# A speech joint kernel on one core: the first batch's projection by w_f as two groups of seven block products

## The chip, the core and the metric

The kernel runs on one core of a Trainium2 chip. The metric is the device time of one execution in microseconds (us). A core has five engines that run side by side, each with its own queue in order: TensorE (PE in the profile, with its weight loads as PEld), VectorE (DVE), ScalarE (ACT), GpSimd (POOL) and SyncE (SP), which here issues the DMA transfers. They wait for one another through semaphores. Matrix products land in PSUM, in eight banks; everything else is in SBUF.

## What is computed

```python
B, T, D, K, U = 2, 4000, 512, 5, 8
for i in range(K):                      # first convolution over time, 5 taps
    h = h + einsum("btc,cd->btd", xp[:, i:i+T, :], w1[i])
h = gelu(h)[:, ::2, :]                  # every second step is kept: 2000
for i in range(K):                      # second convolution
    f = f + einsum("btc,cd->btd", hp[:, i:i+T1, :], w2[i])
f = gelu(f)[:, ::2, :]                  # 1000 steps
fe = einsum("btd,de->bte", f, w_f)      # the projection of this case
ge = einsum("bud,de->bue", g, w_g)
j = tanh(fe[:, :, None, :] + ge[:, None, :, :])
out = einsum("btud,dv->btuv", j, w_o)   # 2 x 1000 x 8 x 512
```

Inputs and output are bf16.

## The kernel before

**Order by a planner.** The body records operations with their reads, writes and an assumed cost in a `Plan` (L69). `edges` (L109) finds which operation must wait for which; `schedule` (L160) and `once` (L228) place them: in each step the engine that can start first takes an operation that is ready. TensorE, SP and Pool take the one recorded first, ACT and DVE the one with the earliest due time. `learn` (L195) moves due times where TensorE has gaps, in up to 150 passes. `emit` (L280) then writes each engine's queue in that fixed order, so on the chip the queues run in order. Operations recorded with `flex` (L90) may go to either of two engines, as the planner finds. `pl.port` marks operations for a rule at L262 to L267: DVE and Pool instructions that are marked do not overlap in the plan, and a marked DVE operation close behind another marked one is charged 0.2 us more.

**Layout.** All features lie with their 512 channels as four blocks of 128 partitions (index k) and time along the free axis. fT[b] holds the second convolution's output of batch b, four blocks of 3 x 334 steps (three residues r, 334 steps each); feT[b] holds fe in f32, four blocks of 1002 steps.

**Stages.** Start-up: `turn` (L575) turns the first rows of x by TensorE and evicts each of four turns in two halves, half 0 on DVE and half 1 on ACT; `direct` (L752) computes the first part of the first convolution from them. Meanwhile `w1part` and `w2part` (L599 and L616) form sums of the convolution weights, on DVE (`tensor_tensor`, `scalar_tensor_tensor`) with scalings on ACT. The convolutions then run as `Triple`s and `Unit`s: a unit is one block of 128 output channels of a part of the time axis, in five steps s1 to s5 of 4 or 8 matmuls of up to 334 columns, with ACT copies (`sd`) and DVE sums between them that free the unit's PSUM bank for its next step. Units 0 to 15 are the first convolution, 16 to 19 the second one of batch 0, 20 to 23 that of batch 1. The main loop (L887) interleaves the steps of neighbouring units and, by `when(slot, ...)`, other work: `load_late` (slot 17) loads w_f, w_g and w_o; `tail_zero` zeroes the end of hT on Pool; `w2part` runs in slots 9 to 13.

**Around the change.** w_f is used by `fe(b, half, m)` (L801): four matmuls of 501 columns into a bank (block m of the output, one half of the time axis), evicted into feT by ACT for odd m and DVE for even m. Batch 0 takes all eight of them in a row behind one convolution step (L1087 to L1092); those of batch 1 stand at the end of the list `conv` of convolution steps that are left, and `piece(n)` takes the next n from that list. The output stage works on j in column blocks of 128. `Seven` (L958) computes four of them, 512 columns of j by 512 outputs, as seven block products: the 2 x 2 blocks of j and of w_o are added and subtracted beforehand (`sums` into ss on DVE or Pool, `wosums` at L843 into tw on Pool), products 1 to 7 of 4 matmuls of 256 columns go to PSUM, some are kept in SBUF (`keep`, into sn), and four outputs are evictions or DVE sums with a kept one. `Plain` (L935) is the direct product of one block of 128. `tanhs` records the ACT tanhs that fill j ahead of the products (rings of 12 and 10 blocks of 256 columns). The loop at L1110 goes over 28 groups of seven; `fill` says what goes between: two convolution steps for each of the first nine groups, one for the next six, then a plain block.

**Buffers.** tw lies over w_g. w_f, w_g and w_o lie over w1_x, so their loads wait for its last use. wv holds f32 sums of w1 from the start-up, ssum and ws those of w2.

Of the kernel before, what the change touches and what calls it, by code (L numbers as in the profile page):

```python
# [12 lines left out]
P = 128  # L13
# [55 lines left out]
class Plan:  # L69
# [158 lines left out]
    def once(self, pred, succ, late, hold):  # L228


        ops, HOP, n = self.ops, self.HOP, len(self.ops)
        left = [len(p) for p in pred]
        ready = list(hold)
        free = {e: 0.0 for e in ("pe", "act", "dve", "pool", "sp")}
        cand = {e: [] for e in free}
        engines = [o.alt or (o.eng,) for o in ops]
        for i in range(n):
            if not left[i]:
                for e in engines[i]:
                    cand[e].append(i)  # L240
        order, where = {e: [] for e in free}, {}
        wire, lock, start, done = 0.0, 0.0, [0.0] * n, [0.0] * n
        for _ in range(n):
            best = None
            for e, c in cand.items():
                if c:
                    t = max(free[e], min(ready[i] for i in c))
                    if best is None or t < best[0]:
                        best = (t, e)
            t, e = best  # L250
            now = [i for i in cand[e] if ready[i] <= t + 0.02]
            i = min(now) if e in ("pe", "sp", "pool") else min(now, key=lambda i: (late[i], i))
            for f in engines[i]:
                cand[f].remove(i)
            order[e].append(i)
            o = ops[i]
            cost = o.cost
            if o.alt:
                where[i], cost = e, o.alt[e][1]
            start[i] = t  # L260
            free[e] = t + cost
            if o.port:  # L262
                if lock > t - 0.2 and e == "dve":
                    free[e] = max(t, lock) + cost + 0.2
                elif lock > t:
                    free[e] = lock + cost
                lock = free[e]  # L267
            done[i] = end = free[e]
            if o.dma:
                wire = max(wire, t + 1.8) + o.wire  # L270
                end = max(wire, t + 2.0) + o.slack
            for s in succ[i]:
                ready[s] = max(ready[s], end + HOP if pred[s][i] else free[e])
                left[s] -= 1
                if not left[s]:
                    for f in engines[s]:
                        cand[f].append(s)
        return max(free.values()), order, start, done, ready, where
# [76 lines left out]
def bass_standalone__seq2seq_rnn_t_joint__speech_kernel(  # L355
# [40 lines left out]
    with ExitStack() as es:  # L396
        cur = [16512]

        def at(name, shape, dtype, offset=None):
            o = cur[0] if offset is None else offset  # L400
            b = Buf(nc, name, shape, dtype, o)
            if offset is None:
                cur[0] = (b.end + 31) // 32 * 32
            return b
# [54 lines left out]
        assert ss[3].end <= xs[2].end and ss[7].end <= xs[1].end  # L459
        tw = at("tw", [4, 2, NT // 2], FP16, wg_sb.end - wg_sb.bytes)  # L460
        assert tw.end <= wg_sb.end
        ps = Psum(es.enter_context(nc.psum_tensor("acc", [P, 8 * NT], FP32)))
        block = es.enter_context(nc.Block(no_gpsimd_drain=True))
        pl = Plan(nc)
# [9 lines left out]
        def tt(eng, o, a, b, op):  # L474
            pl.op(eng, lambda e: e.tensor_tensor(out=o.ap, in0=a.ap, in1=b.ap, op=op), (a, b), (o,),  # L475
                  0.02 + 2.14e-3 * o.ap.free_size() if eng == "pool" else vec_cost(o, (a, b)))
# [98 lines left out]
        def turn(rt, pp, cost):  # L575
            for h in range(2):
                bk = 4 * (rt ^ pp) + 2 * h + 1
                pv = View(psb[:, bk * 1024:bk * 1024 + 512].rearrange("p (r k c) -> p r k c", r=2, k=2), np.array([bk]), True)

                def fn(e, pv=pv, h=h):  # L580
                    for k in range(2):
                        for r in range(2):
                            ins = e.transpose(pv.ap[:, r, k, :], xr[rt].h[:, 2 * r + pp, 2 * h + k, :], ident.h[:, :])
                    return ins
                pl.op("pe", fn, (xr[rt][:], ident[:]), (pv,), cost)
                lo = 16 + 2 * P * rt
                o = eo[pp, 2 * h:2 * h + 2, lo:lo + 2 * P].map(lambda a: a.rearrange("p k (c r) -> p k c r", r=2))
                v = pv.map(lambda a: a.rearrange("p r k c -> p k c r"))
                if h:
                    act(o, v, ACT.Copy)  # L590
                else:
                    pl.op("dve", lambda e, o=o, v=v: e.tensor_copy(out=o.ap, in_=v.ap), (v,), (o,), vec_cost(o, (v,)))
# [42 lines left out]
        class Triple:  # L635
# [5 lines left out]
            def __init__(self, z, off, r, w, out, n=NT3, home={}):  # L641
                self.HOME = {**self.HOME, **home}
                self.z_, self.off, self.r_, self.w, self.out, self.n = z, off, r, w, out, n
# [31 lines left out]
            def product(self, which, m, bank, start):  # L675
                at_z, i = self.HOME[which]
                w, p = self.w[which]
                n = self.n
                mm(ps.cols(bank * NT, n),
                   [(w[p, k, m * P:(m + 1) * P],  # L680
                     self.z_[i, k, self.off:self.off + n] if at_z else self.r_[i, k, 0:n]) for k in range(NK)],
                   start, True, False)
# [118 lines left out]
        def fe(b, half, m):  # L801
            q = NT3 // 2
            v = ps.cols(bank(), 3 * q)
            mm(v, [(wf_sb[k, m * P:(m + 1) * P], fT[b][k, :, half * q:(half + 1) * q]) for k in range(NK)], True, True)
            v = v.map(lambda a: a.rearrange("p (r q) -> p q r", r=3))
            o = feT[b][m, 3 * half * q:3 * (half + 1) * q].map(lambda a: a.rearrange("p (q r) -> p q r", r=3))
            if m % 2:
                act(o, v, ACT.Copy)
            else:
                pl.op("dve", lambda e, o=o, v=v: e.tensor_copy(out=o.ap, in_=v.ap), (v,), (o,), vec_cost(o, (v,)))  # L810

        def slot(j):
            if j < XB:
                return jT, j % RING
            j = (j - XB) % (WIDE + RING)
            return (jX, j) if j < WIDE else (jT, j - WIDE)
# [23 lines left out]
                act(jcols(k, lo, n), feT[b][k, t:t + n], ACT.Tanh, bias=geT[k * BU + v:k * BU + v + 1])  # L840
                lo += n

        def wosums():  # L843
            h = NT // 2
            b11, b12, b21, b22 = (wo_sb[2 * k:2 * k + 2, c * h:(c + 1) * h] for k in range(2) for c in range(2))
            tt("pool", tw[0], b12, b11, sub)
            tt("pool", tw[1], b22, tw[0], sub)
            tt("pool", tw[2], b22, b12, sub)
            tt("pool", tw[3], b21, tw[1], sub)

        def tail_zero(b):
            v = hT[b][2:6, :, HOFF + NT3 - 1:HOFF + NT3]
# [6 lines left out]
        def when(slot, *what):  # L859
            fixed.setdefault(slot, []).extend(what)  # L860

        def steps(slot, i, lo, hi):
            when(slot, *[lambda w=w: trip[i].step(w) for w in STEPS[lo:hi]])
# [18 lines left out]
        when(17, load_late, lambda: tail_zero(1))  # L882
        steps(18, 5, 0, 4)
        steps(19, 5, 4, 13)
        when(20, ge)
        nu = 21
        for t in range(nu):  # L887
# [23 lines left out]
        def take():  # L911
            return free.pop(0)
# [45 lines left out]
        class Seven:  # L958
# [12 lines left out]
            def a(self, r, k):  # L971
                return jcols(slice(2 * k, 2 * k + 2), self.c[r], H)
# [30 lines left out]
            def keep(self, eng, bk):  # L1003
                v = sn[Seven.kept % len(sn)]
                Seven.kept += 1
                evict(eng, v[:], ps.cols(bk * NT, NT))
                return v
# [53 lines left out]
        def tanhs(upto, read, more=0):  # L1061

            while pend:
                v, k = pend[0]
                room = all(owner(j) < 0 or (owner(j) + 1) * JB <= read for j in range(v * T2 // JB, -(-(v + 1) * T2 // JB)))
                if v * T2 >= upto:
                    if not more or not room or v >= U and not far[0]:
                        break
                    more -= 1
                assert room, (v, upto, read)  # L1070
                tanh(*pend.pop(0))
# [8 lines left out]
        def piece(n=1):  # L1080
            for _ in range(n):
                if conv:
                    conv.pop(0)()
                    far[0] = not conv

        wosums()
        first = [lambda h=h, m=m: fe(0, h, m) for m in range(NK) for h in range(2)]  # L1087
        piece()
        for i, f in enumerate(first):
            f()  # L1090
            if i % 2:
                tanhs(0, 0, 1)  # L1092
        piece(3)

        S1 = 15
        gaps = (1, 3, 5, 7)
# [78 lines left out]
```

## Time and profile before

| what | value |
|---|---|
| median of three runs | 254.28 us (253.91 to 254.64) |
| profiled execution, its own time | 253.94 us |
| its span, first to last instruction | 252.2 us |
| TensorE clock granted | 1.000 |
| projection of batch 0, 32 matmuls of 501 columns | 120.35 to 127.17 us |
| w_o sums on Pool, four | 118.31 to 122.9 us, 1.15 us each |
| issue of w_f's load, time to landing | 90.63 us, 3.6 us |
| first output products | 130.01 us; first group of seven about 132 us |
| last tanh ends, last matmul starts | about 232 us, 248.7 us |

A profile page lists busy time by engine, then forty slices of the span with a digit for the busy share of each (9 is 90% or more), then the chain of work that ended last, followed back from the end. Rows of a timeline show start, duration, engine, line of the code, operation, and output <- inputs with their shapes. An instruction's duration runs from its issue, so it may contain a wait for a resource that the profile doesn't name.

### The profile page before, as it was taken

How to read it: one execution, taken by the hardware profiler on the slowest of the kernel's cores; microseconds unless marked ns; L12 is line 12 of the kernel's file. 1: busy time of each engine (PE TensorE's matmuls, PEld its weight loads, DVE VectorE, ACT ScalarE, POOL GpSimd, SP SyncE). 2: the span in 40 equal slices, each digit the busy share in tenths (PEclk: the TensorE clock that was granted, in tenths of full speed). 3: DMA queues.
4: the chain of work that ended last, by engine and by line, in shares of the span. 5: the costliest groups of instructions: out<-in, count | busy, mean ns of one | idle time of the engine just before them, and what ended most of it. 6: DMA issues, size and time to landing. Idle time of an engine off the chain costs nothing.

```text
span 252.2 us, 5270 instructions
## 1 busy us (share of the span) xinstructions
PE 246.4 (98%) x1913; PEld 180.9 (72%) x1919; DVE 209.9 (83%) x342; ACT 210.0 (83%) x352; POOL 103.2 (41%) x107
## 2 busy tenths in 40 slices
PE   7999999999999999999999999999999999999994
PEld 3745977666666666667467878877778878787882
DVE  2699999956999998295546799799899999999783
ACT  4396998859869767884699999999999999998762
POOL 1000000000000000002418889698998999998500
PEclk9999999999999999999999999999999999999999
DMA  6999999989100043000002223332344446555646
GB/s 233 306 229 188 172 142 179 187 148 358 45 0 3 0 143 110 0 1 3 0 0 86 83 87 99 130 108 83 118 137 149 145 135 205 165 167 170 205 149 209
DMA packets 55159, 31.99 MB, mean 127 GB/s; under 512 B 32062, under 2 KB 54878, under 8 KB 55134
## 3 DMA queue, kind: packets, MB, share of 16 engines
q1 hardware_dynamic: 54846, 31.47, 47.6%
q8 instruction: 15, 0.25, 0.4%
q10 hardware_dynamic: 288, 0.20, 0.3%
q14 instruction: 10, 0.08, 0.1%
HBM read 7.86 MB, written 16.38 MB: 96 GB/s over the span
## 4 chain that ended last, share of the span: by engine, by line
PE 87%; DVE 5%; DMA 4%; ACT 1%; issue 1%; SPq 0%; DVEq 0%
PE acc L488 87%; DMA w_sb<-in_w_dram 4%; DVE wu L595 1%; DVE row L475 1%; DVE xa L475 1%; DVE ssum L475 1%; DVE w_t L475 1%; DVE og L475 1%; ACT row L480 0%; DVE w_x L475 0%; ACT w_x L480 0%; ACT sd L480 0%; ACT hT L480 0%; SPq L511 0%; ACT ost L480 0%
## 5 line engine op out<-in xcount | busy, mean ns | idle before, releaser
L475 DVE TENSOR_TENSOR og<-acc,sn 128x512 bf16<-128x512 f32 x84 | 55.6, 683 | 6.4 <-PE acc L488 4.4
L480 ACT ACTIVATE jT<-feT,geT 128x1000 bf16<-128x1000 f32 (+6 forms) x56 | 52.7, 1016 | 0.5 <-DVE feT L810 0.4
L488 PE MATMUL acc<-tw,ss 128*128 128x256 f16 x336 | 46.0, 273 | 0.0
L488 PE MATMUL acc<-row,w_sb 128*128 128x334 bf16 (+2 forms) x224 | 38.8, 296 | 0.0
L488 PEld LDWEIGHTS acc<-tw,ss 128*128 128x128 f16 x336 | 32.6, 98 | 7.8 <-ACT sn L917 0.4
L917 ACT ACTIVATE sn<-acc 128x512 f32<-128x512 f32 x54 | 34.8, 657 | 3.8 <-PE acc L488 3.5
L980 POOL TENSOR_TENSOR ss<-jT 128x512 f16<-128x512 bf16 x23 | 28.8, 1263 | 13.4 <-ACT jT L480 10.8
L488 PE MATMUL acc<-wo_sb,jT 128*128 128x256 bf16 (+1 forms) x187 | 31.5, 292 | 0.3
L488 PEld LDWEIGHTS acc<-row,w_sb 128*128 128x128 bf16 x224 | 21.0, 97 | 8.9 <-DVE acc L595 0.4
L480 ACT ACTIVATE jX<-feT,geT 128x1000 bf16<-128x1000 f32 (+4 forms) x28 | 26.2, 986 | 0.0
L472 POOL MEMSET hT<- 128x8 bf16 (+2 forms) x6 | 0.8, 148 | 61.6 <-ACT hT L480 44.1
L480 ACT ACTIVATE hT<-acc 128x334 bf16<-128x334 f32 (+3 forms) x36 | 15.5, 441 | 9.7 <-PE acc L488 9.7
L488 PEld LDWEIGHTS acc<-wo_sb,jT 128*128 128x128 bf16 x192 | 18.7, 98 | 6.2
L595 DVE SCALAR_TENSOR_TENSOR acc<-acc,sd 128x334 f32<-128x334 f32 (+2 forms) x24 | 11.6, 483 | 13.8 <-PE acc L488 13.7
L480 ACT ACTIVATE sd<-acc 128x334 f32<-128x334 f32 (+2 forms) x48 | 20.4, 433 | 3.2 <-PE acc L488 2.4
L918 DVE COPY sn<-acc 128x512 f32<-128x512 f32 x30 | 20.5, 685 | 2.4 <-PE acc L488 2.4
L475 DVE TENSOR_TENSOR row<-row 128x1336 bf16<-128x1336 bf16 (+2 forms) x24 | 19.0, 795 | 0.0
L980 POOL TENSOR_TENSOR ss<-jX 128x512 f16<-128x512 bf16 x15 | 17.4, 1171 | 1.2 <-ACT jX L480 0.6
L488 PE MATMUL acc<-hT,w_t 128*128 128x334 bf16 x96 | 17.6, 304 | 0.0
L488 PE MATMUL acc<-xp,w_t 128*128 128x334 bf16 (+1 forms) x96 | 17.4, 305 | 0.0
L488 PE MATMUL acc<-xp,w_x 128*128 128x334 bf16 (+1 forms) x96 | 16.9, 305 | 0.0
L488 PE MATMUL acc<-eo,w_sb 128*128 128x468 bf16 (+2 forms) x96 | 16.2, 328 | 0.6 <-ACT eo L480 0.6
(111 smaller groups left out, 511.2 us busy)
## 6 DMA issues: line engine op xcount, KB each, us to landing
out_dram<-og SPq DMA_DIRECT2D x98, 128.0 KB, 2.0
w_sb<-in_w_dram SPq DMA_DIRECT2D x10, 512.0 KB, 5.5
out_dram<-ost SPq DMA_DIRECT2D x10, 128.0 KB, 2.2
xr<-in_x_dram SPq DMA_DIRECT2D x2, 512.0 KB, 4.6
wf_sb<-in_w_f_dram SPq DMA_DIRECT2D x1, 512.0 KB, 3.6
wg_sb<-in_w_g_dram SPq DMA_DIRECT2D x1, 512.0 KB, 4.6
wo_sb<-in_w_o_dram SPq DMA_DIRECT2D x1, 512.0 KB, 5.7
xp<-in_x_dram SPq DMA_TRANSPOSE x18, 4.9
```

What stands on the lines that cost most here:

```text
L472: pl.op("pool", lambda e: e.memset(v.ap, 0.0), (), (v,))
L475: pl.op(eng, lambda e: e.tensor_tensor(out=o.ap, in0=a.ap, in1=b.ap, op=op), (a, b), (o,), 0.02 + 2.14e-3 * o.ap.free_size() if eng == "po ...
L480: pl.op("act", lambda e: e.activation(o.ap, i.ap, func, scale=scale, bias=0.0 if bias is None else bias.ap), rd, (o,), o.ap.free_size() * ...
L488: ins = e.matmul(o.ap, lhsT=l.ap, rhs=r.ap, start=start and n == 0, stop=stop and n == len(pairs) - 1, skip_group_check=not check)
L595: pl.op(eng, lambda e: e.scalar_tensor_tensor(out=o.ap, in0=a.ap, scalar=f, in1=b.ap, op0=ALU.mult, op1=add), (a, b), (o,), vec_cost(o, (a ...
L917: pl.flex({"act": (lambda e: e.activation(o.ap, v.ap, ACT.Copy), 0.05 + n * 0.833e-3), "dve": (lambda e: e.tensor_copy(out=o.ap, in_=v.ap) ...
L918: "dve": (lambda e: e.tensor_copy(out=o.ap, in_=v.ap), 0.065 + n * 1.04e-3)}, (v,), (o,))
L980: fn = lambda e, o=S[i], x=x, y=y, op=op: e.tensor_tensor(out=o.ap, in0=x.ap, in1=y.ap, op=op)
```

## The change

Batch 0's projection no longer runs as eight `fe` calls. Two objects of a new class `FeSeven` compute it as 2 x 2 blocks: the rows are the two halves of the time axis (168 steps of each of three residues, overlapping by two steps), the inner blocks are halves of the 512 channels, and the columns are halves of the 512 outputs; t = 0 or 1 picks one block of 128 within each half. Each object has seven products of 2 matmuls of 504 columns, three kept results (kf, in f32 over ssum and ws) and four outputs. Two sets of sums go in: `fsums` on DVE from fT into sf (bf16, over row[0], four sums of 1008 elements), and `wsums(twf, wf_sb)` on Pool from w_f into twf (f16, over wv, four sums of 512 elements), recorded in slot 18 of the main loop, right after the loads. `wosums` becomes `wsums(tw, wo_sb)`; with `pl.hold` it waits for the last feature sum.

The steps of the remaining convolution that are recorded ahead of the output stage go from four to nine: piece(2), the first products, piece(3), the rest, piece(4). The same steps are then missing from the fill of the later groups. At the start-up, half 0 of the last turn goes to ACT instead of DVE. In the planner a marked operation directly behind another marked one of the same engine is no longer charged for the port.

```diff
-        wire, lock, start, done = 0.0, 0.0, [0.0] * n, [0.0] * n
+        wire, lock, owner, start, done = 0.0, 0.0, None, [0.0] * n, [0.0] * n
...
             if o.port:
-                if lock > t - 0.2 and e == "dve":
+                if owner != e and lock > t - 0.2 and e == "dve":
                     free[e] = max(t, lock) + cost + 0.2
-                elif lock > t:
+                elif owner != e and lock > t:
                     free[e] = lock + cost
-                lock = free[e]
+                lock, owner = free[e], e
...
+        QH = NT3 // 2 + 1
+        twf = at("twf", [4, 2, NT // 2], FP16, wv[2].end - wv[2].bytes)
+        sf = at("sf", [4, 2, 3, QH], BF16, xt_off + 8192)
+        kf = [at(f"kf{i}", [3, QH], FP32, v.end - v.bytes) for i, v in enumerate(ssum + ws[:2])]
...
-                if h:
+                if h or rt and pp:
                     act(o, v, ACT.Copy)
...
+        def fhalf(b, r, k):
+            q0 = r * (NT3 - QH)
+            return fT[b][k, :, q0:q0 + QH]
+
+        def fsums(b):
+            a = lambda r, k: fhalf(b, r, slice(2 * k, 2 * k + 2))
+            pl.port = True
+            tt("dve", sf[0], a(1, 0), a(1, 1), add)
+            tt("dve", sf[1], sf[0], a(0, 0), sub)
+            tt("dve", sf[2], a(0, 0), a(1, 0), sub)
+            tt("dve", sf[3], a(0, 1), sf[1], sub)
+            pl.port = False
+
+        class FeSeven:
...
+            def product(self, i, bk, start):
+                h, lo = NT // 2, self.t * P
+                rhs = {1: lambda k: fhalf(self.b, 0, k), 2: lambda k: fhalf(self.b, 0, 2 + k),
+                       4: lambda k: fhalf(self.b, 1, 2 + k)}.get(i)
+                if rhs is None:
+                    si = {5: 0, 6: 1, 7: 2, 3: 3}[i]
+                    rhs = lambda k: sf[si, k]
+                lhs = {1: lambda k: wf_sb[k, lo:lo + P], 2: lambda k: wf_sb[2 + k, lo:lo + P],
+                       3: lambda k: wf_sb[2 + k, h + lo:h + lo + P]}.get(i)
+                if lhs is None:
+                    ti = {5: 0, 6: 1, 7: 2, 4: 3}[i]
+                    lhs = lambda k: twf[ti, k, lo:lo + P]
+                mm(ps.cols(bk * NT, 3 * QH), [(lhs(k), rhs(k)) for k in range(2)], start, True, False)
...
+            def keep(self, bk):
+                v = kf[FeSeven.kept % len(kf)]
+                FeSeven.kept += 1
+                evict(None, v[:].map(lambda a: a.rearrange("p r q -> p (r q)")), ps.cols(bk * NT, 3 * QH))
+                return v
+
+            def out(self, r, c, bk, v=None):
...
+                if v is None:
+                    evict(None, o, p)
+                else:
+                    tt("dve", o, p, v[:].map(cut), add)
+
+            def p1(self):
+                self.A = take()
+                self.product(1, self.A, True)
+                self.s1 = self.keep(self.A)
+
+            def p2(self):
+                bk = take()
+                self.product(2, bk, True)
+                self.out(0, 0, bk, self.s1)
+                free.append(bk)
...
+            def p6(self):
+                self.product(6, self.A, False)
+                self.u2 = self.keep(self.A)
+
+            def p7(self):
+                self.product(7, self.A, False)
+                self.out(1, 1, self.A, self.d5)
...
-        def wosums():
+        def wsums(tw, w):
             h = NT // 2
-            b11, b12, b21, b22 = (wo_sb[2 * k:2 * k + 2, c * h:(c + 1) * h] for k in range(2) for c in range(2))
+            b11, b12, b21, b22 = (w[2 * k:2 * k + 2, c * h:(c + 1) * h] for k in range(2) for c in range(2))
+            pl.port = True
             tt("pool", tw[0], b12, b11, sub)
             tt("pool", tw[1], b22, tw[0], sub)
             tt("pool", tw[2], b22, b12, sub)
             tt("pool", tw[3], b21, tw[1], sub)
+            pl.port = False
...
         steps(19, 5, 4, 13)
+        when(18, lambda: wsums(twf, wf_sb))
...
-        wosums()
-        first = [lambda h=h, m=m: fe(0, h, m) for m in range(NK) for h in range(2)]
-        piece()
-        for i, f in enumerate(first):
-            f()
-            if i % 2:
-                tanhs(0, 0, 1)
+        piece(2)
+        f0, f1 = FeSeven(0, 0), FeSeven(0, 1)
+        f0.p1()
+        f0.p2()
+        fsums(0)
+        pl.hold = [pl.ops[-1].idx]
+        wsums(tw, wo_sb)
+        pl.hold = []
+        f1.p1()
+        f0.p5()
+        f1.p2()
+        f0.p6()
+        f1.p5()
+        f0.p7()
+        f0.p3()
+        f0.p4()
+        tanhs(0, 0, 1)
         piece(3)
+        f1.p6()
+        f1.p7()
+        f1.p3()
+        f1.p4()
+        tanhs(0, 0, 3)
+        piece(4)
```

In the built program's queues, Pool has the four w_f sums ahead of the zeroing of hT's tail; ACT has the scaling of the last w2 block ahead of a bank copy `sd` that stood ahead of it before; the eight calls' 32 matmuls become 28, with 44 more convolution matmuls between them and the first group of seven than before.

More of the change, by code (lines that the diff above doesn't have):

```diff
@@ L461, in bass_standalone__seq2seq_rnn_t_joint__speech_kernel @@
         assert tw.end <= wg_sb.end
+        QH = NT3 // 2 + 1
+        twf = at("twf", [4, 2, NT // 2], FP16, wv[2].end - wv[2].bytes)
+        sf = at("sf", [4, 2, 3, QH], BF16, xt_off + 8192)
+        kf = [at(f"kf{i}", [3, QH], FP32, v.end - v.bytes) for i, v in enumerate(ssum + ws[:2])]
+        assert twf.end <= wv[3].end and sf.end <= xt[0].end and 3 * QH <= NT
         ps = Psum(es.enter_context(nc.psum_tensor("acc", [P, 8 * NT], FP32)))
@@ new lines, in bass_standalone__seq2seq_rnn_t_joint__speech_kernel, with __init__, p5, p3 @@
+        class FeSeven:
+            def __init__(self, b, t):
+                self.b, self.t = b, t
+            def product(self, i, bk, start):
[11 more added lines that the diff above has]
+                mm(ps.cols(bk * NT, 3 * QH), [(lhs(k), rhs(k)) for k in range(2)], start, True, False)
+            kept = 0
+            def keep(self, bk):
[4 more added lines that the diff above has]
+            def out(self, r, c, bk, v=None):
+                q = NT3 // 2
+                cut = lambda a: a[:, :, r:r + q].rearrange("p r q -> p q r")
+                p = ps.cols(bk * NT, 3 * QH).map(lambda a: cut(a.rearrange("p (r q) -> p r q", r=3)))
+                o = feT[self.b][2 * c + self.t, 3 * r * q:3 * (r + 1) * q].map(lambda a: a.rearrange("p (q r) -> p q r", r=3))
+                if v is None:
[11 more added lines that the diff above has]
+                free.append(bk)
+            def p5(self):
+                self.D = take()
+                self.product(5, self.D, True)
+                self.d5 = self.keep(self.D)
+            def p6(self):
[4 more added lines that the diff above has]
+                self.out(1, 1, self.A, self.d5)
+            def p3(self):
+                self.product(3, self.D, False)
+                self.out(0, 1, self.D, self.u2)
+                free.append(self.D)
+            def p4(self):
+                self.product(4, self.A, False)
+                self.out(1, 0, self.A)
+                free.append(self.A)
```

## The prediction

> **What bounds the kernel now.** I read the first page from the top: busy time, the slices, then the chain of waits.
>
> ```profile
> span 252.2 us, 5270 instructions
> PE 246.4 (98%) x1913; PEld 180.9 (72%) x1919; DVE 209.9 (83%) x342; ACT 210.0 (83%) x352; POOL 103.2 (41%) x107
> ...
> PE   7999999999999999999999999999999999999994
> ...
> DVE  2699999956999998295546799799899999999783
> ...
> PE 87%; DVE 5%; DMA 4%; ACT 1%; issue 1%; SPq 0%; DVEq 0%
> ```
>
> TensorE is busy in every slice but the first and last, and holds 87% of the chain. So a matmul taken away shortens the kernel, and a stall put into TensorE's queue lengthens it, each one for one, unless the planner has another matmul ready. Next I cut the span into the stretches that the change touches (columns: length, then PE, PEld, DVE, ACT, POOL busy with counts, clock, DMA share, GB/s).
>
> ```profile
> 84.00:94.40 10.40, 10.40 (x75) 7.07 (x74) 10.40 (x19) 6.76 (x14) 0.00 (x0) 1.00 0.24 81
> 94.40:100.20 5.80, 5.80 (x43) 3.97 (x41) 5.50 (x12) 4.27 (x9) 0.00 (x0) 1.00 0.40 129
> 100.20:105.40 5.20, 5.20 (x39) 3.57 (x37) 0.01 (x1) 5.13 (x7) 0.17 (x1) 1.00 0.00 2
> ...
> 120.30:127.00 6.70, 6.70 (x34) 3.04 (x33) 3.65 (x6) 4.87 (x8) 2.55 (x3) 1.00 0.00 0
> ```
>
> The last row is the projection that the change rewrites: DVE and ACT have room there. The first two are where its new Pool work lands: Pool is empty, but DVE is full until 100.2, with the sums of the second convolution's weights. Then the DMA issues (time of issue 90.63, 3.6 us to landing for w_f), and for what happens when Pool and DVE work at once, the timeline of the output stage, and all DVE sums into `ss` (ns min/median/max):
>
> ```profile
> 152.17 1.16 POOL L980 TENSOR_TENSOR ss<-ss,jT 128x512 f16<-128x512 f16 x1
> ...
> 152.21 1.40 DVE L980 TENSOR_TENSOR ss<-jT,ss 128x512 f16<-128x512 bf16 x1
> ...
> 153.28 1.34 POOL L980 TENSOR_TENSOR ss<-jT 128x512 f16<-128x512 bf16 x1
> ```
>
> ```profile
> L980 DVE TENSOR_TENSOR ss<-jT x13: 415/462/1373, 127.1 to 237.0; 128x512 f16<-128x512 bf16 x13
> L980 DVE TENSOR_TENSOR ss<-jT,ss x5: 409/775/1397, 145.1 to 167.3; 128x512 f16<-128x512 bf16 x5
> ```
>
> One DVE sum takes 0.42 us alone. The one at 152.21 was issued 0.04 us behind a Pool sum and ended at 153.61, 0.28 us after that Pool sum (153.33): it stood for the whole Pool instruction, and the Pool sum behind it took 1.34 instead of 1.16. The DVE rows that read PSUM show nothing of the kind (the 84 `og` sums have a mean of 683 ns beside a busy Pool). Last, the stretch where the new Pool sums fall:
>
> ```profile
> 95.99 0.68 DVE L475 TENSOR_TENSOR ssum<-w_sb 128x512 f32<-128x512 bf16 x1
> 96.59 0.42 DVE L475 TENSOR_TENSOR w_t<-w_sb 128x512 bf16<-128x512 bf16 x1
> ...
> 97.52 0.42 DVE L475 TENSOR_TENSOR w_t<-w_sb 128x512 bf16<-128x512 bf16 x1
> ```
>
> ```profile
> 98.42 0.44 ACT L480 ACTIVATE sd<-acc 128x334 f32<-128x334 f32 x1
> ...
> 98.91 0.63 ACT L480 ACTIVATE w_sb<-w_sb 128x512 bf16<-128x512 bf16 x1
> ```
>
> ```profile
> 100.08 0.73 PE L488 MATMUL acc<-row,w_t 128*128 128x334 bf16 x4
> ```
>
> The ACT copy `sd` at 98.42 frees the bank into which TensorE writes at 100.08, so it has about 1.2 us to spare. The scaling `w_sb` behind it waits for the DVE sums `w_t` of the last weight block.
>
> **The change part by part**, against the profiled execution (253.94 us: span 252.2 and 1.7 around it; the median 254.28 lies 0.34 above).
>
> *1. Fewer matmuls.* Before, the 32 matmuls of 501 columns run from 120.35 to 127.17, 6.82 us. After, 28 of 504 columns: 14,112 columns for 16,032, so 6.00 us. **-0.8 us**. That weights in f16 against features in bf16 cost nothing shows in `tw,jT` and `wo_sb,jT`: 0.60 us for four in both.
>
> *2. Feature sums, keeps and recombination.* Four DVE sums of 1008 bf16 elements: the 704-element row takes 0.52 and the 1336-element one 0.85, so 0.7 each, 2.7 us. Six keeps and eight outputs replace eight evictions, six more of 0.68 (the `feT` row): 4.1 us, most on DVE. The stretch 117 to 132.2 has 9.2 us of DVE idle (3.3+3.05+2.9), more when five convolution steps join it, so the volume is covered. Latency isn't wholly: I followed the built order with these durations. The first step behind `p2` waits for the DVE read behind the first sum (0.1); `p7` waits for the ACT keep of `p6` (0.1); and in ACT's queue two 1.05 us tanhs stand before copies that free convolution banks (0.1 and 0.4). In all 0.7 us where before had one stall of 0.2: **+0.45**, ends 0 and 1.0.
>
> *3. w_o sums behind the feature sums.* Four Pool sums of 1.15, from about 123.4 to 128. They were wanted at 132.18 and now at about 138, since the five steps moved ahead of the first group are 44 more matmuls of 0.142 (6.3 us). DVE then reads PSUM, which the rows show unharmed. SP's queue keeps its issues and their order. 0; if the cover is gone, at most one Pool sum, 1.2.
>
> *4. Convolution steps moved.* They only move, but the output groups from the ninth on lose their filling. Such a group has 28 matmuls of 0.109 = 3.05 us of TensorE against seven evictions of about 0.6 (start to start) and 2 tanhs of 1.05: 6.3 us over two engines, 3.15 each, so the tanhs' lead of several groups (they end at 232, TensorE at 249) must pay. Before, two such groups at 184 to 190 lose about 0.1 us between them. Six or seven: **+0.3**, ends 0 and 1.0.
>
> *5. One start-up eviction from DVE to ACT, and a new port rule in the planner.* ACT idles 2.06 us there; DVE's chain of weight sums, full from 12 to 36, starts 0.6 earlier. TensorE's weight loads wait 0.36 and 0.50 us there for ACT copies, in a new order now. **-0.3**, ends -0.9 and +0.3. The rule itself changes the split of `ss` sums by one (29 to 28 on DVE): 0.
>
> *6. w_f sums near the load.* Four Pool sums, free to start when w_f lands: 90.63 + 3.6 = 94.2, say 94.4. The zeroing of hT's tail stands behind them on Pool (100.78 before, due about 100.4 now: no harm). From 94.4 DVE has six sums of two SBUF operands left, and the planner charges its port rule only for marked operations, which these are not. By the rows above each Pool sum holds one DVE sum back, and the DVE sum then holds the next Pool sum. Start to start these DVE sums take 0.60 (f32) or 0.34 (bf16): the third scaling sum, due 94.7, runs 95.5 to 96.1; `w_sb`, due 96.5, runs 97.2 to 97.8; the first `w_t` of the last block ends at 99.2; `ssum` at 100.9; the second `w_t` at 101.25, where before it was 97.86. In the changed order ACT's scaling `w_sb` stands *ahead* of the copy `sd`. So the scaling runs at 101.35, the copy ends at 102.3, and TensorE's step due at 100.08 starts at 102.45. **+2.4 us**. The next step, due 2.4 later at 103.6, has its DVE read by 102.9. DVE catches up in its idle 5.2 us; TensorE, always full, does not. No row shows an f32 DVE sum beside a Pool sum. If only the bf16 ones are held, the second `w_t` is some 0.9 late and the cost is 0 to 0.5; if w_f lands 1 us later all four still hit and it is 3. Ends 0 and 3.3; the nearest rows, same engine and operation with both operands in SBUF, speak for 2.4.
>
> The Trainium skill (SBUF — State Buffer, Who interferes with whom) states that a DVE instruction with two SBUF inputs contends with a GpSimd instruction that reads SBUF, whoever comes second blocking fully. The `ss` rows agree (1.40 against 0.42 us), and by that rule the f32 sums are held too.
>
> Sum: -0.8 + 0.45 + 0.3 - 0.3 + 2.4 = +2.05. 253.94 + 2.05 = 256.0 for the profiled execution, **256.3** for the median.
>
> **The rivals.** *A, no harm from Pool:* f32 sums are not held, or w_f lands so early that DVE gets through. For it: no row shows an f32 sum held. Against: the same operation is held in 16 bits. Then -0.35: 253.9; with the start-up gain at its end and no latency loss, 252.9. This is the side of not slower; it decides if the second `w_t` ends before about 99.2, so that scaling and copy are done by 100.1. *B, the hold is real but swallowed:* the planner's order leaves TensorE slack I did not see and the stall is at most 0.7, net +0.3: 254.6. Against: TensorE's queue is in order and its next step needs that very bank. *C, the thinned groups become the bound as well:* six groups at 3.6 instead of 3.05 add 3.3 less the 0.3 counted, and the time is 257.8 with half of that paid by the tanhs' lead. For it: ACT is busy 41 of 42 us from 190 to 232. Against: DVE and ACT have 7 us free after 232.
>
> **How the numbers follow.** Forecast 0.68, A 0.15, B 0.07, C 0.10. What a measurement here can't tell from no change is about 0.3%, 0.76 us: 253.5 to 255.0. The forecast (own range 255.1 to 257.5) and C are slower: 0.78. A is half faster (0.08), half the same; with B the same is 0.14. The range from 254.2 to 257.8 leaves out most of A and the far end of C.
>
> **What would show it.** Right: the four `twf` rows on Pool near 94.4 to 100.5, DVE sums of 1 us or more between them, a TensorE idle of about 2 us near 100 ended by ACT `sd`, and 28 matmuls of 504 columns. Wrong: those DVE rows at 0.42 and 0.68, or a TensorE without a gap there; or gaps of 0.2 and more in each group from the ninth on.

## The result, and the profile after

| | before | changed |
|---|---|---|
| median of the runs (4 and 4) | 254.34 us | 256.81 us |
| lowest to highest | 253.91 to 254.64 | 256.70 to 257.10 |
| profiled execution, its span | 253.94, 252.2 | 256.83, 255.0 |
| ratio, 95% interval | | 1.0100, 1.0083 to 1.0118 |

The change costs 2.5 us; 256.3 was forecast, in a range of 254.2 to 257.8. The page of the changed kernel, the lines that were shown of before:

```profile
span 255.0 us, 5268 instructions
PE 246.7 (97%) x1909; PEld 180.6 (71%) x1915; DVE 217.4 (85%) x346; ACT 211.7 (83%) x356; POOL 109.3 (43%) x113
...
PE   8999999999999997999999999999999998999994
...
DVE  2699998947999999298867988899899997899783
...
PE 71%; DVE 15%; ACT 8%; issue 4%; DVEq 0%; ACTq 0%
```

TensorE's busy time has hardly changed (246.7 for 246.4), but two digits inside its row are no longer 9, near 100 and near 210 us, and DVE and ACT hold more of the chain of waits (15 and 8% for 5 and 1%). The same stretches as before, and a new one (length, then PE, PEld, DVE, ACT, POOL busy with counts, clock, DMA share, GB/s):

```profile
84.00:94.40 10.40, 10.40 (x75) 7.07 (x74) 10.40 (x20) 6.76 (x14) 0.07 (x1) 1.00 0.23 78
94.40:100.20 5.80, 5.80 (x42) 3.77 (x39) 5.80 (x6) 2.89 (x6) 5.43 (x4) 1.00 0.40 134
100.20:107.00 6.80, 4.86 (x34) 3.15 (x34) 2.82 (x6) 5.71 (x9) 0.17 (x1) 1.00 0.00 1
119.00:132.00 13.00, 13.00 (x93) 7.52 (x92) 9.59 (x17) 8.08 (x17) 4.54 (x4) 1.00 0.00 0
...
207.00:212.60 5.60, 4.43 (x37) 3.35 (x36) 5.60 (x6) 4.47 (x12) 3.47 (x4) 1.00 0.46 142
```

From 94.4 to 100.2 DVE gets through 6 instructions in the time that took 12 before, with Pool busy beside it; from 100.2 to 107 TensorE stands for 1.9 us. The projection's stretch (119 to 132) has TensorE full.

**The gap near 100 us.** Timelines of Pool, DVE, ACT and TensorE there (start, duration, then in brackets the idle time before and what ended it):

```profile
94.33 2.73 POOL L480 TENSOR_TENSOR twf<-wf_sb 128x512 f16<-128x512 bf16 x2 [33.47 <-DMA wf_sb<-in_w_f_dram]
97.02 2.89 POOL L480 TENSOR_TENSOR twf<-wf_sb,twf 128x512 f16<-128x512 bf16 x2
```

```profile
94.70 1.33 DVE L600 SCALAR_TENSOR_TENSOR ws<-w_sb,ws 128x512 f32<-128x512 bf16 x1
...
96.38 1.23 DVE L480 TENSOR_TENSOR w_sb<-ssum,w_sb 128x512 bf16<-128x512 f32 x1
97.53 1.37 DVE L480 TENSOR_TENSOR w_t<-w_sb 128x512 bf16<-128x512 bf16 x1
98.82 1.64 DVE L480 TENSOR_TENSOR ssum<-w_sb 128x512 f32<-128x512 bf16 x1
100.38 0.41 DVE L480 TENSOR_TENSOR w_t<-w_sb 128x512 bf16<-128x512 bf16 x1
```

```profile
100.83 0.63 ACT L485 ACTIVATE w_sb<-w_sb 128x512 bf16<-128x512 bf16 x1 [2.94 <-DVE w_t L480]
101.36 0.43 ACT L485 ACTIVATE sd<-acc 128x334 f32<-128x334 f32 x1
...
103.51 2.43 ACT L485 ACTIVATE row<-hT 128x2688 bf16<-128x2688 bf16 x1
105.84 0.77 ACT L485 ACTIVATE sd<-acc 128x334 f32<-128x334 f32 x2
```

```profile
99.51 0.73 PE L493 MATMUL acc<-xp,w_sb 128*128 128x334 bf16 x4
101.85 0.74 PE L493 MATMUL acc<-row,w_t 128*128 128x334 bf16 x4 [1.61 <-ACT sd L485]
...
106.33 0.74 PE L493 MATMUL acc<-row,w_sb 128*128 128x334 bf16 x4 [0.33 <-ACT sd L485]
```

Four Pool sums hold four DVE sums, one each, f32 ones too: 1.23 to 1.64 us where they take 0.4 to 0.7 alone. The second `w_t` comes at 100.38, ACT's scaling waits for it, the copy `sd` stands behind the scaling, and TensorE's step waits for the copy. A row of four such matmuls lasts 0.567 from start to start, so the step was due at 100.08 and is 1.77 late. A second one at 106.33 is 0.49 late: its bank copy stands on ACT behind the long `row` copy, which began at 100.99 before and at 103.51 now. Together 2.26 us.

**The gap near 210 us** was not foreseen. Timelines of DVE, Pool and TensorE:

```profile
204.82 2.47 DVE L480 TENSOR_TENSOR og<-acc,sn 128x512 bf16<-128x512 f32 x4
207.22 3.54 DVE L1073 TENSOR_TENSOR ss<-jT,ss 128x512 f16<-128x512 bf16 x1
210.68 1.87 DVE L480 TENSOR_TENSOR og<-acc,sn 128x512 bf16<-128x512 f32 x3
```

```profile
205.99 2.26 POOL L1073 TENSOR_TENSOR ss<-jT 128x512 f16<-128x512 bf16 x2
208.22 1.15 POOL L1073 TENSOR_TENSOR ss<-ss,jT 128x512 f16<-128x512 f16 x1
209.33 1.14 POOL L1073 TENSOR_TENSOR ss<-jT 128x512 f16<-128x512 bf16 x1
212.97 1.27 POOL L1073 TENSOR_TENSOR ss<-ss,jT 128x512 f16<-128x512 f16 x1 [2.49 <-PE acc L493]
```

```profile
209.65 0.60 PE L493 MATMUL acc<-tw,ss 128*128 128x256 f16 x4
211.42 0.61 PE L493 MATMUL acc<-tw,jT 128*128 128x256 f16 x4 [1.17 <-DVE og L480]
```

One DVE sum of 0.41 us stands for 3.54, behind the Pool sum that ran (207.11 to 208.25) and two more. It ends 0.29 us after Pool's row, which stops at 210.47, where Pool has to wait for TensorE. The `og` reads behind it free TensorE's banks: four matmuls of 256 columns last 0.44, so TensorE was due at 210.09 and is 1.33 late. All other DVE sums of the changed kernel that met a Pool sum got in after the one that ran.

### The profile page after: what moved, and what is told of

Its sections match the earlier page's. It is cut to its first block, busy times and chain, and to the rows that moved or that the text cites. A ratio compares the mean times of both kernels' runs of the same rounds, so it can differ in the third digit from the quotient of the medians.

```text
span 255.0 us, 5268 instructions
## 1 busy us (share of the span) xinstructions
PE 246.7 (97%) x1909; PEld 180.6 (71%) x1915; DVE 217.4 (85%) x346; ACT 211.7 (83%) x356; POOL 109.3 (43%) x113
## 4 chain that ended last, share of the span: by engine, by line
PE 71%; DVE 15%; ACT 8%; issue 4%; DVEq 0%; ACTq 0%
PE acc L493 70%; DVE row L480 4%; ACT row L485 3%; DVE ssum L480 2%; DVE ws L600 2%; DVE hT L480 1%; DVE sd L480 1%; DVE acc L600 1%; ACT sd L485 1%; ACT jT L485 1%; DVE xp L480 1%; DVE w_sb L480 1%; ACT jX L485 1%; DVE w_t L480 1%; PE acc L588 1%
## 5 line engine op out<-in xcount | busy, mean ns | idle before, releaser
L480 DVE TENSOR_TENSOR og<-acc,sn 128x512 bf16<-128x512 f32 x84 | 54.6, 681 | 7.9 <-PE acc L493 6.7
L1010 ACT ACTIVATE sn<-acc 128x512 f32<-128x512 f32 x51 | 32.3, 639 | 2.6 <-PE acc L493 1.7
L1073 POOL TENSOR_TENSOR ss<-jT 128x512 f16<-128x512 bf16 x25 | 29.9, 1210 | 9.4 <-ACT jT L485 5.4
L485 ACT ACTIVATE jX<-feT,geT 128x1000 bf16<-128x1000 f32 (+4 forms) x28 | 25.0, 953 | 0.0
L1011 DVE COPY sn<-acc 128x512 f32<-128x512 f32 x33 | 22.1, 680 | 1.9 <-PE acc L493 1.7
L485 ACT ACTIVATE sd<-acc 128x334 f32<-128x334 f32 (+2 forms) x48 | 19.7, 430 | 3.4 <-PE acc L493 2.8
L1073 POOL TENSOR_TENSOR ss<-jX 128x512 f16<-128x512 bf16 x16 | 18.8, 1189 | 0.1
L493 PE MATMUL acc<-row,w_t 128*128 128x334 bf16 (+2 forms) x96 | 16.5, 294 | 1.8 <-ACT sd L485 1.8
L480 POOL TENSOR_TENSOR twf<-wf_sb 128x512 f16<-128x512 bf16 x2 | 2.7, 1384 | 33.5 <-DMA wf_sb<-in_w_f_dram 33.5
L493 PE MATMUL acc<-wo_sb,ss 128*128 128x256 bf16 x112 | 17.0, 273 | 0.0
```

The costliest lines, as they stand in the source:

```text
L485: pl.op("act", lambda e: e.activation(o.ap, i.ap, func, scale=scale, bias=0.0 if bias is None else bias.ap), rd, (o,), o.ap.free_size() * ...
L493: ins = e.matmul(o.ap, lhsT=l.ap, rhs=r.ap, start=start and n == 0, stop=stop and n == len(pairs) - 1, skip_group_check=not check)
L1010: pl.flex({"act": (lambda e: e.activation(o.ap, v.ap, ACT.Copy), 0.05 + n * 0.833e-3), "dve": (lambda e: e.tensor_copy(out=o.ap, in_=v.ap) ...
L1011: "dve": (lambda e: e.tensor_copy(out=o.ap, in_=v.ap), 0.065 + n * 1.04e-3)}, (v,), (o,))
L1073: fn = lambda e, o=S[i], x=x, y=y, op=op: e.tensor_tensor(out=o.ap, in0=x.ap, in1=y.ap, op=op)
```

## The experiments

The kernel before ran beside each batch; where it ran more than once, its medians were 254.22 to 254.35 us. All variants of the whole kernel but one differ from it by less than 2%, so each ratio is given with its 95% interval.

**Is it the w_f sums on Pool?** First, the same sums on DVE:

```diff
-        def wsums(tw, w):
+        def wsums(tw, w, eng="pool"):
...
-            tt("pool", tw[0], b12, b11, sub)
+            tt(eng, tw[0], b12, b11, sub)
...
-        when(18, lambda: wsums(twf, wf_sb))
+        when(18, lambda: wsums(twf, wf_sb, "dve"))
```

> The changed kernel with the four w_f sums on DVE instead of Pool; TensorE's and ACT's queues are the same, instruction by instruction. Theory (Pool's w_f sums hold the DVE sums of the second convolution's weights, and TensorE waits for ACT behind them): the gaps of 1.77 and 0.49 us near 100 and 106 go, the four sums take 0.42 us each, 256.8 - 2.3 = 254.5 us. If the second gap (1.2 us near 210, a DVE sum held for three Pool sums) was a matter of chance and goes too, 253.2. Rival (the loss comes from the new projection and the thinned groups, the sums are harmless): no change, 256.8.

Measured: 254.51 us (10 runs), ratio to before 1.0014 (1.0005 to 1.0024). TensorE's queue is that of the changed kernel, and the step is on time:

```profile
99.40 0.73 PE L493 MATMUL acc<-xp,w_sb 128*128 128x334 bf16 x4
99.97 0.73 PE L493 MATMUL acc<-row,w_t 128*128 128x334 bf16 x4
```

The gap near 100 is gone and with it 2.30 us; the one near 210 is still there, 1.33 us. Then the sums alone, put into the kernel before, where nothing reads them:

```diff
+        twf = at("twf", [4, 2, NT // 2], FP16, wv[2].end - wv[2].bytes)
...
-        def wosums():
+        def wosums(tw=tw, wo_sb=wo_sb):
...
+        when(18, lambda: wosums(twf, wf_sb))
```

> The kernel before, and the four w_f sums added on Pool in the same slot; nothing reads them, and every other queue is unchanged. Theory: the DVE sums near 95 to 100 take 1.2 us and more, ACT's copy is late, TensorE waits 2.0 to 2.6 us near 100: 254.3 + 2.3 = 256.6 us. Rival (sums harmless): 254.3.

Measured: 256.17 us (4 runs), ratio 1.0085 (1.0068 to 1.0101). So the sums alone cost 1.9 us, 0.4 less than expected; TensorE starts 1.60 late at 101.73 and 0.43 late at 106.15. Here ACT's copy stands behind another scaling, `w_t<-ssum`, whose DVE sum was held 1.64 us. Third, the sums on Pool but behind the DVE sums of w2:

```diff
+        def wf_late():
+            pl.hold = list(w2_dve)
+            wsums(twf, wf_sb)
+            pl.hold = []
...
-        when(18, lambda: wsums(twf, wf_sb))
+        when(18, wf_late)
```

> The changed kernel with the Pool's w_f sums held until the DVE sums of the second convolution's weights are done. Theory: the sums run in the 5 us in which DVE has nothing to do, about 100 to 105; no gap near 100; 254.5 us, or 253.2 if the gap near 210 goes with it. The planner reorders some steps near 103 to 112, which may move it by 0.3. Rival: 256.8.

Measured: 254.57 us (10 runs), ratio 1.0010 (1.0001 to 1.0020); no gap near 100, the other 1.32. It is neither the engine nor the work but the moment: five us later the same Pool sums cost nothing (the planner also puts some convolution steps between 103 and 112 us in another order). The changed kernel once more beside them:

> The changed kernel once more, for a second profile. If the gap of 1.2 us near 210 is fixed by the order of the queues, a DVE sum is held for three Pool sums (3.5 us) there again; if it is chance, the same DVE sum is held for one (at most 1.4 us) and the time is some 1.2 us shorter, 255.6. The gaps near 100 and 106 are there in both cases.

257.05 us (one run), both gaps again (2.07 and 0.49; 1.34, with the DVE sum at 3.55).

**The held sum near 210 us.** I took the DVE sum away by giving the seventeenth group's sums to Pool, in the kernel with the w_f sums on DVE:

```diff
-                    pl.flex({k: alt[k] for k in (("dve", "pool"))}, (x, y), (S[i],))
+                    pl.flex({k: alt[k] for k in (("pool",) if self.n == 17 else ("dve", "pool"))}, (x, y), (S[i],))
```

> The changed kernel with two edits: the w_f sums on VectorE (as in the run that gave 254.5 us), and all sums of the seventeenth group of seven products on GpSimd alone, so that no VectorE sum of that group can be held. Theory (the gap of 1.33 us near 207 us comes from the VectorE sum ss<-jT,ss that stands 3.54 us while three GpSimd sums run): the gap goes, the time is 254.5 - 1.2 = 253.3 us, between 252.9 and 253.7, below the kernel before. Rival 1 (the gap comes from the order of the groups there, whoever makes the sums): the gap stays within 0.4 us of 1.33 and the time is 254.3 to 254.8. Rival 2 (the fourth sum on GpSimd makes the group's sums later than its first product): a new wait of TensorE for GpSimd at the seventeenth group, 254.5 or more.

Measured: 267.91 us (4 runs), ratio 1.0536 (1.0518 to 1.0553). The theory and the first rival fell; the second has a time that fits, but not the wait. DVE's and TensorE's timelines, and the row of granted clocks of the page:

```profile
205.46 13.97 DVE L1073 TENSOR_TENSOR ss<-jT 128x512 f16<-128x512 bf16 x1
219.35 0.68 DVE L480 TENSOR_TENSOR og<-acc,sn 128x512 bf16<-128x512 f32 x1
```

```profile
207.26 0.60 PE L493 MATMUL acc<-tw,ss 128*128 128x256 f16 x4
220.09 1.04 PE L493 MATMUL acc<-tw,jT 128*128 128x256 f16 x4 [12.22 <-DVE og L480]
```

```profile
PEclk9999999999999999999999999999999856999999
```

Another DVE sum now stands 13.97 us, through 13 Pool sums, to the end of Pool's row at 219.15; TensorE waits for DVE, 12.4 us by its matmuls. So the sum taken away was not special, and the hold ends only when Pool runs out of work. Another run, planned before this result was known, tried the point of a Pool sum at which a DVE sum is issued (0.11 us after a start for the 3.54 us; the 13.97 us were issued 0.75 after one, which already speaks against it): 118 Pool sums in a row, with DVE sums at many points.

> Leaves the whole computation out; the output isn't the reference's. GpSimd runs 118 sums of 512 elements one behind another (1.15 us each in the kernel); beside them VectorE runs sums of two SBUF operands, 30 of 16 bits and 12 with a 32-bit operand, each behind a copy from PSUM of another length, so that they come at many points of a GpSimd sum, and 8 sums of PSUM and SBUF. Theory A (a held VectorE sum gets in at the end of the GpSimd sum that runs, unless it is issued 0.10 to 0.15 us after that one's start, then it stands for three): nearly all of the 42 stand for 0.3 to 1.5 us, and the few issued 0.10 to 0.15 us after a start for 3 us or more. Rival B (the point of issue has nothing to do with it): sums of 3 us or more come at other points too, or none comes at any. Rival C (a chain of GpSimd sums without a pause holds VectorE to its end): one VectorE sum stands for tens of us. The PSUM and SBUF sums aren't held by any: 0.6 us each as without GpSimd beside them.

All DVE sums by operation (ns min/median/max): two 16-bit operands, one of 32 bits, PSUM and SBUF:

```profile
L62 DVE TENSOR_TENSOR d<-a,b x33: 424/805/1416, 9.2 to 68.1; 128x512 f16<-128x512 bf16 x33
```

```profile
L63 DVE TENSOR_TENSOR d<-f,b x15: 692/998/1266, 10.5 to 86.9; 128x512 f32<-128x512 f32 x15
```

```profile
L64 DVE TENSOR_TENSOR d<-acc,f x11: 691/691/692, 12.7 to 96.0; 128x512 f32<-128x512 f32 x11
```

None stood for 3 us, also none of those issued 0.09, 0.13 and 0.17 us after a start (1.34, 1.29 and 1.26 us); A fell, and C too; B, that the point of issue doesn't matter, stands. But here a DVE sum came after every one or two Pool sums. I then counted, for every held DVE sum of the kernels, how many Pool sums had run in the row before: no more than 6 where it got in after one, 22 or 23 in the changed kernel and its variants where it stood to the end. So a row's length was tried next: VectorE reads only PSUM until the row has got to some n, then issues one sum.

> Leaves the whole computation out; the output isn't the reference's. Fourteen trials. In each GpSimd runs n + 8 sums of 512 elements without a pause (1.11 us from start to start), and VectorE, which has only instructions with a PSUM operand until then (copies, or sums of PSUM and SBUF), issues one sum of two SBUF operands when about n of them are done; n is 3, 6, 9, 12, 16, 20, 26 behind copies and 6, 12, 20, 26 behind sums with PSUM. Then three more with n = 26: one with a second such VectorE sum half-way, one in which GpSimd pauses half-way, and one plain. Theory (what counts is how long GpSimd has run without a pause: in the kernels a VectorE sum got in after one GpSimd sum where that was up to 5 us, and stood to the end of GpSimd's row where it was 24.6 to 25.8 us): a threshold between n = 5 and n = 22, below it the VectorE sum takes 0.4 to 1.6 us, above it 8 to 9 us, to the end of the row; with the VectorE sum or the pause half-way it takes 0.4 to 1.6 us if half the row is below the threshold; the plain one again 8 to 9 us. Rival (length has nothing to do with it; something else of the kernel near 207 us, say its DMAs or TensorE's traffic): all take 0.4 to 1.6 us.

Two of the trials, n = 12 and n = 16, on DVE's timeline:

```profile
73.98 1.20 DVE L91 TENSOR_TENSOR d<-a,b 128x512 f16<-128x512 bf16 x1
```

```profile
101.40 9.18 DVE L91 TENSOR_TENSOR d<-a,b 128x512 f16<-128x512 bf16 x1
```

The theory holds, with the threshold between 13 sums (15.2 us) and 16 (17.7 us). Another run told whether it counts time or instructions:

> Leaves the whole computation out; the output isn't the reference's. As the run with fourteen trials, to tell what the threshold counts: rows of GpSimd sums of 512 elements (n = 13, 14, 15), of 256 (n = 14, 18, 22, 26, 30, 34; some 0.55 us each) and of 1024 (n = 5, 6, 7, 8, 10, 14, 17; some 2.2 us each), with one VectorE sum of two SBUF operands at about the n-th, 8 more behind it. So far a VectorE sum got in after one GpSimd sum where the row had run for 15.2 us (13 sums before it), and stood to the row's end at 17.7 us (16 sums). Theory T (it counts time): with 256 elements the VectorE sum gets in at n up to 26 (some 15 us) and stands to the end (4 us or more) from n = 34 on, with 1024 it gets in at n = 6 and below and stands (17 us) from n = 8 on. Theory I (it counts GpSimd's instructions): with 256 it stands from n = 18 on, with 1024 it gets in at n up to 10 and stands at 17 alone.

On either side of the threshold, 13 and 14 Pool sums of 512 elements done, then 16 of 256 and 10 of 1024:

```profile
25.55 1.11 DVE L84 TENSOR_TENSOR d<-a,b 128x512 f16<-128x512 bf16 x1
...
51.09 8.77 DVE L84 TENSOR_TENSOR d<-a,b 128x512 f16<-128x512 bf16 x1
...
116.08 6.01 DVE L84 TENSOR_TENSOR d<-a,b 128x512 f16<-128x512 bf16 x1
...
372.71 1.24 DVE L84 TENSOR_TENSOR d<-a,b 128x512 f16<-128x512 bf16 x1
```

All trials of both (counted from the two traces, one execution each; the Pool sum that runs isn't counted):

```
elements  Pool sums done in the row  row had run  VectorE sum took
512       3, 6, 8, 12, 13            3 to 14.7    0.6 to 1.5 us: one Pool sum
512       14, 14, 16, 20, 26         15.9 to 29   8.8 to 9.3 us: to the row's end
512       13 since a VectorE sum     15.2         0.8 us: one
512       11 since a Pool pause      13.0         0.6 us: one
256       13                         8.2          0.9 us: one
256       16, 20, 23, 26, 31         10.5 to 19.5 6.0 to 7.2 us: to the row's end
1024      5, 6, 7, 8, 10             11.1 to 21.9 1.0 to 1.6 us: one
1024      14, 18                     30.9, 37.5   15.1, 14.7 us: to the row's end
```

Theory T fell: 256 elements stand at 10.5 us, 1024 get in at 21.9. It counts Pool's instructions: up to 13 done in an unbroken row the VectorE sum gets in after the one that runs; from 14 on it stands until the row ends. The step from 13 to 14 itself is seen with 512 elements; with 256 it lies between 13 and 16, with 1024 between 10 and 14. Theory I named 17 alone for 1024 elements; 14 stood as well, which the count of 14 explains.

**The same in the kernel.** If so, one DVE sum half-way cures it. The changed kernel, the thirteenth group's third sum put on DVE:

```diff
-                    pl.flex({k: alt[k] for k in (("dve", "pool"))}, (x, y), (S[i],))
+                    pl.flex({k: alt[k] for k in (("dve",) if (self.n, i) in ((13, 2),) else ("dve", "pool"))}, (x, y), (S[i],))
```

> The changed kernel with one edit: the third sum of the thirteenth group of seven products is put on VectorE, which comes about half-way in the unbroken row of GpSimd sums from some 182 to 210 us and cuts it into rows of 11 to 12 us. Theory (a VectorE sum of two SBUF operands stands to the end of GpSimd's row once the row has run for more than 15.2 to 17.7 us): every VectorE sum there gets in after one GpSimd sum (under 1.5 us), the gap of 1.33 us near 210 us goes, the gap near 100 us stays: 256.8 - 1.3 = 255.5 us, between 255.2 and 255.9. Rival (the gap near 210 us is of the order of the groups, not of the length of the row): the gap stays within 0.4 us of 1.33, and the time is 256.5 to 257.2.

Measured: 255.58 us (5 runs), ratio 1.0048 (1.0032 to 1.0063); TensorE has no gap near 210 us, and that near 100 stays. With this edit the planner also moves some products near 195 us to an earlier place; the order near the gap is the same. Then with the w_f sums on DVE, cut once and cut twice:

> The same edit in the kernel with the w_f sums on VectorE (254.5 us), so that neither gap is left. Theory: 254.5 - 1.3 = 253.2 us, between 252.9 and 253.6, below the kernel before by 0.3 to 0.5%. Rival: 254.2 to 254.8 us, the gap still there.

> As the run before, with the third sum of the fifteenth group on VectorE too, which cuts the row of GpSimd sums a second time. Theory: nothing more to gain, since no row is above the threshold: within 0.4 us of the run before. Rival (what helps is less work for GpSimd, not the length of the row): another 0.3 us or more below it.

Measured: 253.32 us (5 runs), ratio 0.9960 (0.9945 to 0.9975), and 253.28 us (6 runs), 0.9957 (0.9941 to 0.9973). DVE's two sums in the former:

```profile
192.52 0.66 DVE L1073 TENSOR_TENSOR ss<-jX 128x512 f16<-128x512 bf16 x1
...
205.09 0.55 DVE L1073 TENSOR_TENSOR ss<-jT,ss 128x512 f16<-128x512 bf16 x1
```

With no more than ten Pool sums in the row before it, each gets in after one, and TensorE has no gap there. The second cut adds nothing: it is the row's length, not Pool's load. Both kernels are 0.4% faster than before, beyond the interval, and the four times agree as a sum of two terms:

| | w_f sums on Pool near the load | on DVE |
|---|---|---|
| row of Pool sums whole | 256.81 | 254.51 |
| cut once | 255.58 | 253.32 |

**The start-up eviction** was put back on DVE, in the kernel with the late w_f sums:

```diff
-                if h or rt and pp:
+                if h:
```

> The changed kernel with the w_f sums late (the run that gave 254.57 us), and without the move of one start-up eviction from VectorE to ScalarE. It sizes that move. The prediction's -0.3 us: the time is 254.87 us, between 254.7 and 255.0, and the losses of TensorE between 20 and 60 us rise from some 0.9 to 1.2 to 1.4 us. Rival (the move is worth nothing, since the start-up varies by itself): 254.4 to 254.7 us and the same losses between 20 and 60 us.

Measured: 254.58 us (11 runs), ratio 1.0017 (1.0008 to 1.0027), beside 1.0010 with the move. The time is the rival's. By the ratios the move brings 0.2 us, by the medians nothing, and the intervals overlap. TensorE's losses from 20 to 60 us (start to start of its matmuls, less 0.567 us for four of 334 columns and the same rate for others) do rise, 0.90 to 1.24 us, but they run from 0.90 to 1.42 in the profiles of the other kernels with the move and from 1.10 to 1.35 in those without, and the first 10 us vary by 0.7. The planner also orders the steps between 26 and 44 us differently here. So what the move is worth is not settled: nothing fits, and so do the 0.3 predicted. With the planner's new port rule undone, the changed kernel has the same queues on every engine.

## Why the prediction was right where it was, and what it missed

The place, the sign and the chain of step 6 came out; the sum came out 0.5 us low, because two terms were too high by 0.75 us together and one of 1.2 us was missing.

*Step 1, -0.8.* The projection has 1,920 columns fewer; at the 0.567 us that four times 334 columns take from start to start, that is -0.81.

*Step 2, +0.45.* About nothing: between 119 and 132 us TensorE is full, its longest gap 0.05 us. The latencies that I added up by hand cost it nothing.

*Step 3, 0.* Right: the w_o sums end at 130.2 us, the first group's products that read them start at 139.9 and wait for nothing.

*Step 4, +0.3.* The groups from the ninth on lose no more than before (0.2 to 0.4 us between 160 and 200 in both, a size at which missing records count; later the only gap over 0.25 us is that near 210). Why no such loss came, the tanhs' lead or not, was not tried. Rival C, that these groups become the bound by the work of DVE and ACT, fell with it.

*Step 5, -0.3 and 0 for the rule.* The rule's 0 is right; the size of the move is open, within the step's bounds.

*Step 6, +2.4.* Right in mechanism; the size is in part luck. Predicted: the second `w_t` over at 101.25, the step at 102.45; they came at 100.79 and 101.85, so the first gap is 0.6 shorter. The step behind it lost nothing, as forecast, but a later one, which the prediction didn't follow, lost 0.49 us behind ACT. The rows show 2.26; the pairs of kernels that differ in where these sums run give 2.30, 2.24 and 2.26. Rival A is excluded: the f32 sums are held (1.64 for 0.68). The Trainium skill's rule on this (SBUF — State Buffer, Who interferes with whom), that whichever engine comes second blocks fully, agrees with these rows. Rival B is excluded too: TensorE lost 2.26 us there, not at most 0.7.

*What was missing: +1.2.* The step took one Pool sum to hold one DVE sum, whatever the row before it, and nothing in the profile of before says otherwise: no DVE sum there comes after more than 6 Pool sums. The rule just named has the lock held for one instruction; it has no such end of a row, and here the measurement decides. The changed order runs 25 Pool sums from 182.58 to 210.47 with no DVE sum of two SBUF operands getting in between. By the two pairs it costs 1.23 and 1.19. That the convolution steps moved ahead made this row is argued from the order, not tried by itself.

The sum of what was measured is -0.81 + 2.26 + 1.21 = +2.66; the change measured +2.47, so all else, the start-up among it, comes to -0.2. The forecast's +0.75 for steps 2 and 4 made up for most of the missing 1.2: the time was nearer than its parts, and that is luck.

## What to carry to other kernels

Before work is moved onto an idle engine, look at what its neighbour does in those microseconds: the same four GpSimd sums cost 2.3 us at 94 us and nothing at 99. Where an unbroken row of GpSimd sums grows past some 13, a VectorE sum of two SBUF operands behind them may wait for the whole rest, so cut the row with a VectorE sum or a pause. And price a wait by rows of the profile that are like it in what ran before them, not in the operation alone; when a cure makes things much worse, as 13.97 us did here, its trace tells more than the one that was to be cured.

## What the runs showed of the hardware that was not expected

- A VectorE sum of two SBUF operands gets in after one GpSimd sum if 13 or fewer have run in the row, and stands to the row's end from 14 on (rows of 256, 512 and 1024 elements; 16 trials below, 15 above). A VectorE sum that got in (one trial, and the kernels whose row was cut), or a pause of GpSimd (one trial), starts the count again. Only `tensor_tensor` sums were tried, and what keeps the count, no run shows.
- VectorE's reads of PSUM beside the same GpSimd rows aren't touched: 691 or 692 ns in all 11, eight of them beside Pool sums.
- After the 12.2 us in which it stood, TensorE's matmuls of 256 columns took 213 ns from start to start instead of 109 until 224.8 us, another 2.3 us lost; the granted clock, in the row shown above, is 8, 5 and 6 tenths in the slices from 206 to 226 us. The Trainium skill (TensorE: Matmul & The Clock Gate, Part 1) has the clock halved after an idle window and released after some 3.4 us of work; the row here is 4.7 us long.
